# Expert products in four-chunk blocks with column halves, second matrices in 2 KB runs, small steps of selection moved

## The chip, the cores and the metric

The kernel runs on one NeuronCore of one Trainium2 chip. The metric is the device time of one execution in microseconds (us), less is better. The profile is one further execution, recorded instruction by instruction.

## The reference

A gated recurrence runs over 4 sequences of 5056 steps and 256 channels: `f = lb + (1-lb)*sigmoid(f_logit)`, `h = f*h + (1-f)*x`, and every `h` is kept. The 20224 rows of `h` are then tokens of a mixture of 8 experts: `logits = h @ w_gate`, a token goes to the expert with the largest logit, and of each expert's tokens only the 80 with the largest gate probability are kept. A kept token's output row is `gate * (relu(h @ w1[e]) @ w2[e])` (256 to 1024 to 256, float32); every other output row is zero. So 20.7 MB of output are nearly all zeros, 41.4 MB of `x` and `f_logit` are read, and 16.8 MB of expert matrices.

## The kernel before, in words

The order of the instructions on each engine is the order of the program text; nothing is rearranged later. All large transfers are issued from SP's queue, in that order, and with eight completion lanes in turn: a transfer waits until the one eight places ahead has landed.

**The recurrence** (loop at L421) goes through 40 units (10 groups of 512 steps x 4 sequences). A unit loads `f_t` and `x_t` (512 KB each, pool `ld`, four buffers each), takes the sigmoid on ScalarE, multiplies on GpSimd (`enter`, L259), turns both to channels by transposes on TensorE (`to_channels`, L268), makes the decay on ScalarE (L278), scans on VectorE (L286) and makes the logits on TensorE (`logits`, L301), in four column tiles of 32. Zeros of the output are written by copies from an already cleared part of the output to the rest (`clear`, L169), a few among the loads, many after them.

**Selection** (from the end of the loop to L630) makes exponentials (L355), sums on GpSimd (`halved`, L369), masked probabilities (`worth`, L383), transposes of them (`candidates`, L389 and L395), maxima (`peaks`, L400) and then the lists of tokens on VectorE. `busy` (L183) issues matrix products whose result nobody reads. `marks`, `gm` and other tiles lie in the pool `gsm`, which is opened with `ld` and closed with it after the selection's first part. The tile `fresh` in PSUM collects the maxima; two copies by ScalarE (L487, L490) read it before VectorE's search (L560) does.

**Experts** (`experts`, L676). Each expert's two matrices come in halves of 512 KB into a ring of six buffers (`wring`), which takes over the space of `ld` alone: w1 halves at L514 (rows of 2 KB) and w2 halves at L518 (rows of 1 KB). Six are issued before selection's end, with clears among them; each of the other 26 is issued when a half six places ahead has been used up (`more`, L704), 21 of them with a clear of 256 KB behind it. Tokens' columns are gathered out of `h_all` by copies with addresses from registers (L693). Then comes the loop over 64 steps (8 experts x 8 chunks of 128 hidden channels): a step's `hidden` (L725) multiplies a chunk of w1, the stationary operand of 128 columns, with 80 tokens; after four chunks comes a relu (L734); `result` (L740) adds a chunk's product with w2 (256 columns streamed), and in `steps` it runs LAG = 6 steps behind `hidden`, one chunk of each in turn. Each float32 product is two loads and two products on TensorE in the trace. `finish` (L755) scales by the gate, `scatter` (L758) writes 80 rows of the output from GpSimd's queue; scatters wait until all clears are issued and landed. At the very end a register with a flag is loaded on every engine (L804), and a branch (L806) skips a slow exact path.

Of the kernel before, what the change touches and what calls it, by code (L numbers as in the profile page):

```python
# [18 lines left out]
P = 128  # L19
TOP = 8  # L20
# [15 lines left out]
def kernel(  # L36
# [167 lines left out]
    with tc.tile_pool(name="ld", bufs=4) as ld, \  # L204
         tc.tile_pool(name="gsm", bufs=1) as gsm:

        xs, fs, sts, uts, sps, ups, lgs, lss, lts, exs, gms, sms = ({} for _ in range(12))

        zero = gsm.tile([P, ZC], F32, name="zero", tag="ls")

        def setup():
            early = gsm.tile([P, 1], F32, name="early", tag="mx")
            nc.scalar.activation(early, ones, ACT.Sigmoid)
            col_i = gsm.tile([P, P], I32, name="col_i", tag="eq")
            nc.gpsimd.iota(col_i, pattern=[[1, P]], base=0, channel_multiplier=0)
            nc.gpsimd.memset(zero, 0.0)
            col_f = gsm.tile([P, P], F32, name="col_f", tag="gm", bufs=2)
            whole = row_i[:, 0:1]
            for i, (shift, mask) in enumerate(((shift_c, E - 1), (0, C - 1), (2, 1), (0, R - 1),
                                               (0, 2 * R), (0, W - 1))):  # L220
                nc.vector.tensor_scalar(row_i[:, ds(1 + i, 1)], whole, shift, mask,
                                        ALU.arith_shift_right, ALU.bitwise_and)
            nc.vector.tensor_copy(row_f[:, :7], row_i[:, :7])
            res, void = spot_of[:, 0:1], spot_of[:, 1:2]
            nc.vector.scalar_tensor_tensor(out=res, in0=row_f[:, 4:5], scalar=2.0,
                                           in1=row_f[:, 3:4], op0=ALU.mult, op1=ALU.add)
            nc.vector.tensor_tensor(res, res, row_f[:, 5:6], ALU.add)
            nc.vector.tensor_scalar(void, row_f[:, 6:7], float(run(n_grp - 1) // R), GONE,
                                    ALU.is_ge, ALU.mult)
            nc.vector.tensor_copy(col_f, col_i)  # L230
            nc.vector.tensor_scalar(place, col_f[:, :C], row_f[:, 2:3], None, ALU.is_equal)
            nc.vector.tensor_scalar(mine, col_f[:, :E], row_f[:, 1:2], None, ALU.is_equal)
            nc.vector.tensor_scalar(before, col_f, row_f[:, 0:1], None, ALU.is_gt)
            nc.vector.tensor_single_scalar(col_i, col_i, shift_c, op=ALU.arith_shift_right)
            nc.vector.tensor_copy(col_f, col_i)
            nc.vector.tensor_scalar(mates, col_f, row_f[:, 1:2], None, ALU.is_equal)
            nc.vector.tensor_tensor(before, before, mates, ALU.mult)
            busy(psu, 9, "up")
            lb_t = plg.tile([P, DC], F32, name="lb_t", tag="lt")
            nc.tensor.transpose(lb_t, lb, ident[:DC, :DC])  # L240
            nc.vector.tensor_scalar(omlb, lb_t, -1.0, 1.0, ALU.mult, ALU.add)
            nc.vector.tensor_scalar(nomlb, lb_t, 1.0, -1.0, ALU.mult, ALU.add)

        def gates():
            for o in range(DC):
                nc.scalar.activation(wg[:, o], wg[:, o], ACT.Identity, scale=omlb[:, ds(o, 1)])

        def load(n):
            g, b = divmod(n, B)
            fs[n] = ld.tile([P, R, D], F32, name="f_t", tag="f_t")  # L250
            nc.sync.dma_start(out=fs[n], in_=tiles(f_logit, b, g))
            xs[n] = ld.tile([P, R, D], F32, name="x_t", tag="x_t")
            nc.sync.dma_start(out=xs[n], in_=tiles(x, b, g))

        def gate(n):
            s_t = sts[n] = fs.pop(n)
            nc.scalar.activation(s_t, s_t, ACT.Sigmoid, scale=-1.0)  # L257

        def enter(n):  # L259
            u_t = uts[n] = xs.pop(n)  # L260
            (nc.gpsimd if n else nc.vector).tensor_tensor(u_t, sts[n], u_t, ALU.mult)  # L261

        def to_channels(n, src, dst, pool, tag, in_time):
            for o in range(DC):
                ps = dst[n, o] = pool.tile([P, G], F32, name=tag, tag=tag)
                for r in range(R):
                    at = ps[:, r::R] if in_time else ps[:, ds(r * P, P)]
                    nc.tensor.transpose(at, src[n][:, r, ds(o * P, P)], ident)  # L268
            del src[n]

        def columns(n, o):
            g, b = divmod(n, B)
            return h_all[:, b, o, ds(first(g), size(g))]


        def decay(n):
            for o in range(DC):
                nc.scalar.activation(columns(n, o).rearrange("c (p r) -> c p r", r=R),  # L278
                                     sps.pop((n, o)).rearrange("c (r p) -> c p r", r=R)
                                     [:, lead(n // B) // R:],  # L280
                                     ACT.Identity, scale=nomlb[:, ds(o, 1)], bias=1.0)

        def scan(n):
            for o in range(DC):
                h = columns(n, o)
                nc.vector.tensor_tensor_scan(  # L286
                    h, h, ups.pop((n, o))[:, lead(n // B):],
                    columns(n - B, o)[:, size(n // B - 1) - 1:] if n >= B else 0.0,
                    ALU.mult, ALU.add)


        def logits(n):
            g, b = divmod(n, B)
            k = run(g)
            if b == 0:
                lgs[g] = plg.tile([P, B, P], F32, name="lg", tag="lg")
            for o in range(DC):
                h = columns(n, o)
                h = h.rearrange("c (m r two) -> c r m two", r=R, two=2)
                for r in range(R):  # L300
                    nc.tensor.matmul(lgs[g][ds(r * LC, LC), b, :k], wg[:, o], h[:, r],  # L301
                                     start=o == 0, stop=o == DC - 1, skip_group_check=True)

        def aside(g, lo=0, hi=B):
            k = run(g)
            if lo == 0:
                lss[g] = gsm.tile([P, B, P], F32, name="ls", tag="ls")
                if k < P:
                    nc.gpsimd.memset(lss[g][:, :, k:], 0.0)
            nc.scalar.copy(lss[g][:, lo:hi, :k], lgs[g][:, lo:hi, :k])  # L310

        def by_token(g):
            ls = lss.pop(g).rearrange("p b t -> p (b t)")
            lts[g] = plg.tile([P, R, P], F32, name="lt", tag="lt")
            for j in range(R):
                nc.tensor.transpose(lts[g][:, j], ls[:, j::R], ident)

        def shifts(g):
            return cand[:, ds(g * P, P)].rearrange("p (c e) -> p c e", e=E)

        marks = gsm.tile([P, n_grp, C, E], BF16, name="marks")

        full = [P, C, E]

        def maxima(g):
            lg = lts.pop(g).rearrange("p j (r e) -> p (j r) e", e=LC)[:, :, :E]
            mx = gsm.tile([P, C], F32, name="mx", tag="mx")
            nc.vector.tensor_reduce(mx, lg, AX.X, ALU.max)
            nc.vector.tensor_tensor(shifts(g), lg, mx.unsqueeze(2).broadcast_to(full),
                                    ALU.subtract)  # L330

        def shifted(g):
            by_token(g)
            maxima(g)

        def chosen(g):
            eq = gsm.tile([P, C, E], F32, name="eq", tag="eq")
            nc.vector.scalar_tensor_tensor(
                out=eq, in0=shifts(g), scalar=0.0,
                in1=revexp.unsqueeze(1).broadcast_to(full), op0=ALU.is_ge, op1=ALU.mult)  # L340
            pick = gsm.tile([P, C], F32, name="pick", tag="pick")
            nc.vector.tensor_reduce(pick, eq, AX.X, ALU.max)
            return eq, pick

        def mark(g, eq, pick, engine):
            engine.tensor_tensor(marks[:, g], eq, pick.unsqueeze(2).broadcast_to(full),
                                 ALU.subtract)

        def choice(g, engine):
            mark(g, *chosen(g), engine)  # L350

        def exponentials(g0, g1, aside=False):
            sh = cand[:, ds(g0 * P, (g1 - g0) * P)]
            exs[g0] = gsm.tile([P, P], F32, name="ex", tag="ex") if aside else sh
            nc.scalar.activation(exs[g0], sh, ACT.Exp)  # L355
# [531 lines left out]
```

## Time and profile before

| | us |
|---|---|
| median of 3 runs (218.59 to 222.11) | 218.66 |
| the profiled execution, whole | 217.36 |
| its span, first to last instruction | 215.5 |
| TensorE busy / VectorE / GpSimd / ScalarE | 187.8 / 150.7 / 139.1 / 131.4 |
| SP's transfers, packet time as a share of 16 DMA engines | 94.9% |

The span is the stretch that the rows below divide; 1.9 us lie around it. "Busy" is the union of the engine's instructions; a busy TensorE is not TensorE at its peak.

### The profile page before, as it was taken

The numbers are of one execution on the slowest core, as the hardware profiler recorded it, in microseconds if no ns is written. First come the engines' busy times: TensorE is split into PE (matmuls) and PEld (weight loads), VectorE is DVE, ScalarE is ACT, GpSimd is POOL, SyncE is SP. The second block draws the span as 40 slices with busy tenths as digits, with TensorE's granted clock in tenths as the row PEclk, the third lists the DMA queues.
The fourth block names the chain that finished last, engine by engine and source line by source line (L and its number), as shares of the span: only waits on it lengthen the run. The fifth ranks groups of instructions, "written<-read, shape, count | busy, mean of one in ns | idle before, by whom it ended". The sixth has DMA issues, their size and how long they took to land. (4 is left out here: it accounts for less than half of the span.)

```text
span 215.5 us, 5581 instructions
## 1 busy us (share of the span) xinstructions
PE 187.8 (87%) x1878; PEld 158.2 (73%) x1878; DVE 150.7 (70%) x479; ACT 131.4 (61%) x370; POOL 139.1 (65%) x279
## 2 busy tenths in 40 slices
PE   7888689999999999999999767798969899889980
PEld 7677478788878787878788546798857687668850
DVE  5687659999998989898989768945777524510010
ACT  4776588879888888888878623559524443611100
POOL 3484887989898989898888761049966623000741
PEclk9999999999999999999999999999999999999996
DMA  6999999999999999999999899999999999999910
GB/s 218 414 399 416 417 422 415 418 414 426 409 417 414 419 411 417 411 407 424 409 408 395 283 378 363 386 320 400 338 368 410 392 406 405 404 401 397 319 57 24
DMA packets 28825, 80.55 MB, mean 374 GB/s; under 512 B 3058, under 2 KB 11380, under 8 KB 26484
## 3 DMA queue, kind: packets, MB, share of 16 engines
q1 hardware_dynamic: 28400, 79.45, 94.9%
q0 software_dynamic: 384, 0.66, 1.0%
q8 instruction: 17, 0.28, 0.5%
q14 instruction: 20, 0.16, 0.2%
q10 hardware_dynamic: 4, 0.00, 0.0%
HBM read 78.39 MB, written 21.36 MB: 463 GB/s over the span
## 5 line engine op out<-in xcount | busy, mean ns | idle before, releaser
L261 POOL TENSOR_TENSOR x_t<-f_t,x_t 128x1024 f32<-128x1024 f32 x39 | 92.3, 2374 | 16.4 <-DMA x_t<-in_x_dram 11.0
L286 DVE TENSOR_TENSOR_SCAN h_all<-h_all,up 128x512 f32<-128x512 f32 (+1 forms) x80 | 94.7, 1242 | 7.5 <-ACT h_all L278 6.5
L278 ACT ACTIVATE h_all<-sp,nomlb 128x512 f32<-128x512 f32 (+1 forms) x80 | 50.0, 676 | 12.6 <-PE sp L268 12.5
L257 ACT ACTIVATE f_t<-f_t 128x1024 f32<-128x1024 f32 x40 | 42.4, 1061 | 9.3 <-DMA f_t<-in_f_logit_dram 9.2
L268 PE MATMUL up<-ident,x_t 128*128 128x128 f32 x320 | 42.0, 274 | 4.7 <-POOL x_t L261 4.7
L725 PEld LDWEIGHTS h_ps<-xt,w_sb 128*128 128x128 f32 x256 | 36.8, 191 | 12.5 <-DVE xt L701 3.5
L268 PE MATMUL sp<-ident,f_t 128*128 128x128 f32 x320 | 44.6, 283 | 0.1
L268 PEld LDWEIGHTS sp<-ident,f_t 128*128 128x128 f32 x320 | 35.0, 143 | 8.2 <-issue 5.5
L268 PEld LDWEIGHTS up<-ident,x_t 128*128 128x128 f32 x320 | 35.6, 141 | 6.8 <-POOL x_t L261 6.7
L725 PE MATMUL h_ps<-xt,w_sb 128*128 128x80 f32 x256 | 36.8, 269 | 4.0 <-DMA w_sb<-in_moe_w_dram 3.1
L740 PE MATMUL y_ps<-w_sb,hid 128*80 128x256 f32 x128 | 37.3, 381 | 1.3 <-DMA w_sb<-in_moe_w_dram 1.3
L693 POOL COPY xe<-h_all 128x8 uint8 x192 | 26.5, 198 | 16.4 <-issue 6.5
L301 PE MATMUL lg<-h_all,wg 128*32 128x128 f32 (+1 forms) x640 | 26.5, 282 | 5.3 <-ACT ls L310 3.9
L693 DVE COPY xe<-h_all 128x8 uint8 x256 | 20.8, 163 | 11.5 <-issue 11.4
L734 ACT ACTIVATE hid<-h_ps 128x320 f32<-128x320 f32 x16 | 7.0, 436 | 32.3 <-PE h_ps L725 32.3
L301 PEld LDWEIGHTS lg<-h_all,wg 128*32 128x32 f32 x640 | 15.4, 108 | 12.3 <-ACT ls L310 6.8
L693 ACT COPY xe<-h_all 128x8 uint8 x192 | 20.2, 193 | 5.5 <-issue 3.5
L758 POOL DMA_INDIRECT out_dram<-y,goal x8 | 7.5, 938 | 23.8 <-DMA w_sb<-in_moe_w_dram 19.7
L755 DVE TENSOR_SCALAR y<-y_ps,gsl 80x256 f32<-80x256 f32 x8 | 3.8, 477 | 22.6 <-PE y_ps L740 22.6
L183 PE MATMUL warm<-ident 128*128 128x128 f32 x128 | 17.2, 298 | 1.4 <-POOL ident masks.py:199 1.4
L183 PEld LDWEIGHTS warm<-ident 128*128 128x128 f32 x128 | 16.6, 212 | 1.5 <-POOL ident masks.py:199 1.4
L740 PEld LDWEIGHTS y_ps<-w_sb,hid 128*80 128x80 f32 x128 | 14.8, 152 | 2.2 <-issue 1.4
(126 smaller groups left out, 91.9 us busy)
## 6 DMA issues: line engine op xcount, KB each, us to landing
f_t<-in_f_logit_dram SPq DMA_DIRECT2D x40, 512.0 KB, 6.1
x_t<-in_x_dram SPq DMA_DIRECT2D x40, 512.0 KB, 6.5
w_sb<-in_moe_w_dram SPq DMA_DIRECT2D x32, 512.0 KB, 7.7
out_dram<-out_dram SPq DMA_DIRECT2D x34, 256.0 KB, 7.8
out_dram<-out_dram SPq DMA_DIRECT2D x6, 768.0 KB, 11.6
out_dram<-out_dram SPq DMA_DIRECT2D x4, 1024.0 KB, 12.4
out_dram<-zero SPq DMA_DIRECT2D x4, 256.0 KB, 8.4
out_dram<-out_dram SPq DMA_DIRECT2D x2, 512.0 KB, 7.8
```

Source lines behind the costliest of these rows:

```text
L183: nc.tensor.matmul(warm, ident, ident, start=True, stop=True)
L257: nc.scalar.activation(s_t, s_t, ACT.Sigmoid, scale=-1.0)
L261: (nc.gpsimd if n else nc.vector).tensor_tensor(u_t, sts[n], u_t, ALU.mult)
L268: nc.tensor.transpose(at, src[n][:, r, ds(o * P, P)], ident)
L278: nc.scalar.activation(columns(n, o).rearrange("c (p r) -> c p r", r=R), sps.pop((n, o)).rearrange("c (r p) -> c p r", r=R) [:, lead(n // ...
L286: nc.vector.tensor_tensor_scan(h, h, ups.pop((n, o))[:, lead(n // B):], columns(n - B, o)[:, size(n // B - 1) - 1:] if n >= B else 0.0, AL ...
L301: nc.tensor.matmul(lgs[g][ds(r * LC, LC), b, :k], wg[:, o], h[:, r], start=o == 0, stop=o == DC - 1, skip_group_check=True)
L693: copy(xe[:, :, ds(WORD * (k + j), WORD)], pair(v - HOME))
L725: nc.tensor.matmul(HP[e, i][:, c], w[1, e, i][:, o, ds(c * P, P)], XT[e][:, o], start=o == 0, stop=o == DC - 1, skip_group_check=True)
L734: nc.scalar.activation(HID[e][:, ds(i * CH, CH)], HP.pop((e, i)), ACT.Relu)
L740: nc.tensor.matmul(YP[e], HID[e][:, c], w[2, e, c // CH][:, c % CH], start=c == 0, stop=c == FC - 1)
L758: one = nc.gpsimd.indirect_dma_start(out=out, out_offset=bass.IndirectOffsetOnAxis(ap=goal[:, ds(e, 1)], axis=0), in_=Y.pop(e), in_offset= ...
```

## The change

1. `gsm` is allocated at the other end of the memory, so that `ld` can be released right after the loop; `wring` and the first six weight loads stand there in the program text.
2. The exponentials of eight groups are split into two of four groups, the second one unit later; those of group 8 go to a tile of their own and before the loop's end. Their sum comes ahead of `chosen`. Three idle products (`busy(psu, 3)`) go. The two copies out of `fresh` move behind the first search and its replacement.
3. w2 halves: a partition takes two neighbouring rows (`RUN` = 2, 2 KB) where it took one; so chunk `c` of the hidden channels is every second channel of a block of 256, and `hidden` reads every second column of w1.
4. `hidden` makes each product as two of 64 stationary columns, into PSUM partitions 0 to 63 and 64 to 127. `LAG` is 4, and `steps` does a block of four `hidden` and then a block of four `result`. The order of the weight loads stays the same.
5. The flag is loaded during expert 6 and not at the end.

```diff
-    with tc.tile_pool(name="ld", bufs=4) as ld, \
-         tc.tile_pool(name="gsm", bufs=1) as gsm:
+    gsm = tc.alloc_tile_pool(name="gsm", bufs=1, side="right")
+    ld = tc.alloc_tile_pool(name="ld", bufs=4)
...
             elif n == LAST - 2:
-                exponentials(0, OLD)
+            exponentials(0, HALF)
             elif n == LAST - 1:
                 halved(0, HALF)
+            exponentials(HALF, OLD)
+            exponentials(OLD, OLD + 1, aside=True)
...
+    ld.release()
+    wring = ...; the six first weights(*key) with their clears
...
-        best = chosen(OLD)
-        exponentials(OLD, OLD + 1)
         logits(LAST)
         aside(g, B - 1, B)
+    sums(OLD, OLD + 1)
+    best = chosen(OLD)
...
-        sums(OLD, OLD + 1)
         candidates(0)
-        busy(psu, 3, "up")
         candidates(2)
...
         peaks(HALF, fresh)
-        nc.scalar.copy(cand[:, OLD * P:], fresh[:, NP * TOP:])
-        ...
-        nc.scalar.copy(last_of, eighths)
+    gsm.release()
...
-    LAG = FC - 2
+    LAG = CH
+    HC = P // 2
+    RUN = 2
...
-            nc.sync.dma_start(out=t, in_=w2[e][ds(i * FH, FH)].rearrange(
-                "(c p) d -> p c d", p=P))
+            nc.sync.dma_start(out=t.rearrange("p (h j) d -> p h j d", j=RUN),
+                              in_=w2[e][ds(i * FH, FH)].rearrange(
+                                  "(h p j) d -> p h j d", p=P, j=RUN))
...
         nc.vector.match_replace(out=rest, in_to_replace=vals2[:, :TOP], in_values=fresh,
                                 imm_value=GONE)
+        nc.scalar.copy(cand[:, OLD * P:], fresh[:, NP * TOP:])
+        last_of = consts.tile([P, NP], F32, name="last_of")
+        nc.scalar.copy(last_of, fresh[:, TOP - 1:NP * TOP:TOP])
...
+                h, r = divmod(c, RUN)
                 for o in range(DC):
-                    nc.tensor.matmul(HP[e, i][:, c], w[1, e, i][:, o, ds(c * P, P)], XT[e][:, o],
-                                     start=o == 0, stop=o == DC - 1, skip_group_check=True)
+                    for j in range(0, P, HC):
+                        at = (h * P + j) * RUN + r
+                        nc.tensor.matmul(HP[e, i][ds(j, HC), c],
+                                         w[1, e, i][:, o, at:at + (HC - 1) * RUN + 1:RUN],
+                                         XT[e][:, o], start=o == 0, stop=o == DC - 1,
+                                         skip_group_check=True)
...
-                for s in range(lo, hi):
-                    if s < E * FC:
-                        hidden(s)
-                    if 0 <= s - LAG < E * FC:
-                        result(s - LAG)
+                for s in range(lo, min(hi, E * FC)):
+                    hidden(s)
+                for s in range(max(lo - LAG, 0), hi - LAG):
+                    result(s)
...
+                if e == E - 2 and not again:
+                    flag.append(nc.values_load(doubt, ...))
...
-    unsure = nc.values_load(doubt, ...)
+    unsure = flag[0]
```

## Rows read from the trace of the kernel before

**Rows 1.** The page: GB/s moved in 40 equal slices of the span (5.4 us each).
```profile
GB/s 218 414 399 416 417 422 415 418 414 426 409 417 414 419 411 417 411 407 424 409 408 395 283 378 363 386 320 400 338 368 410 392 406 405 404 401 397 319 57 24
```
**Rows 2.** Stretches: length, engines busy (instructions), granted clock, DMA share, GB/s.
```profile
20.00:100.00 80.00, 74.10 (x923) 62.43 (x921) 72.20 (x81) 65.73 (x92) 69.53 (x35) 1.00 1.02 416
142.00:158.00 16.00, 14.82 (x118) 13.71 (x116) 10.80 (x117) 11.04 (x99) 13.29 (x96) 1.00 0.98 344
158.00:192.00 34.00, 30.32 (x202) 24.30 (x202) 17.22 (x174) 14.18 (x105) 13.21 (x96) 1.00 1.05 403
198.00:205.00 7.00, 7.00 (x51) 5.96 (x50) 0.54 (x2) 0.87 (x2) 4.65 (x5) 1.00 0.92 324
```
**Rows 3.** The chain that ended last, in order of time: start us, us, what.
```profile
146.89 2.90 PE h_ps L725 x24
...
151.57 8.91 DMA w_sb<-in_moe_w_dram
...
183.87 8.46 DMA w_sb<-in_moe_w_dram
...
195.21 0.40 PE h_ps L725 x4
...
206.00 3.04 PE y_ps L740 x14
...
209.07 0.49 DVE y L755
```
**Rows 4.** SP's queue in order of time: start us, us, engine, line, operation.
```profile
148.94 0.37 SPq L518 DMA_DIRECT2D w_sb<-in_moe_w_dram  x1
...
161.13 0.52 SPq L169 DMA_DIRECT2D out_dram<-out_dram  x1
162.56 0.37 SPq L518 DMA_DIRECT2D w_sb<-in_moe_w_dram  x1
163.11 0.52 SPq L169 DMA_DIRECT2D out_dram<-out_dram  x1
164.45 0.37 SPq L514 DMA_DIRECT2D w_sb<-in_moe_w_dram  x1
```
**Rows 5.** The last weight load (L518, 199.1 us): its time to landing.
```profile
DMA to landing us min/median/max: 5.8/5.8/5.8
```
**Rows 6.** TensorE's products and weight loads by time; in brackets idle before, and releaser.
```profile
114.86 0.86 PEld L268 LDWEIGHTS sp<-ident,f_t 128*128 128x128 f32 x8 [0.21 <-issue]
115.69 0.56 PEld L316 LDWEIGHTS lt<-ident,ls 128*128 128x128 f32 x4
117.24 0.61 PE L301 MATMUL lg<-h_all,wg 128*32 128x112 f32 x16
120.12 1.02 PE L301 MATMUL lg<-h_all,wg 128*32 128x112 f32 x32
```
**Rows 7.** Selection by time: exponentials, idle products, VectorE's two waits.
```profile
118.96 1.06 ACT L355 ACTIVATE cand<-cand 128x1024 f32<-128x1024 f32 x1
123.32 0.75 PEld L183 LDWEIGHTS warm<-ident 128*128 128x128 f32 x6
124.92 0.91 DVE L400 MAX8 fresh<-cand 128x8 f32<-128x256 f32 x2 [1.12 <-ACT cand L395]
130.45 0.47 DVE L560 MAX8 vals<-fresh 128x8 f32<-128x288 f32 x1 [0.58 <-ACT last_of L490]
```
**Rows 8.** What SP's queue waited for between 115 and 150 us: total, times, longest.
```profile
SPq L514 <- PE up L268: 4.4, 1, 4.4
SPq L518 <- PE h_ps L725: 4.1, 1, 4.1
```
**Rows 9.** The scatters by time, and TensorE's load of the flag (ns).
```profile
206.65 0.91 POOL L758 DMA_INDIRECT out_dram<-y,goal  x1 [0.30 <-issue]
209.82 0.91 POOL L758 DMA_INDIRECT out_dram<-y,goal  x1 [2.27 <-DVE y L755]
L804 PEldq TENSOR_LOAD <-doubt x1: 694/694/694, 206.6 to 206.6; - x1
```

More of the change, by code (lines that the diff above doesn't have):

```diff
@@ new lines, in gates, with load, gate @@
+    def gates():
+        for o in range(DC):
+            nc.scalar.activation(wg[:, o], wg[:, o], ACT.Identity, scale=omlb[:, ds(o, 1)])
+    def load(n):
+        g, b = divmod(n, B)
+        fs[n] = ld.tile([P, R, D], F32, name="f_t", tag="f_t")
+        nc.sync.dma_start(out=fs[n], in_=tiles(f_logit, b, g))
+        xs[n] = ld.tile([P, R, D], F32, name="x_t", tag="x_t")
+        nc.sync.dma_start(out=xs[n], in_=tiles(x, b, g))
+    def gate(n):
+        s_t = sts[n] = fs.pop(n)
+        nc.scalar.activation(s_t, s_t, ACT.Sigmoid, scale=-1.0)
@@ new lines, in enter, with to_channels, columns @@
+    def enter(n):
+        u_t = uts[n] = xs.pop(n)
+        (nc.gpsimd if n else nc.vector).tensor_tensor(u_t, sts[n], u_t, ALU.mult)
+    def to_channels(n, src, dst, pool, tag, in_time):
+        for o in range(DC):
+            ps = dst[n, o] = pool.tile([P, G], F32, name=tag, tag=tag)
+            for r in range(R):
+                at = ps[:, r::R] if in_time else ps[:, ds(r * P, P)]
+                nc.tensor.transpose(at, src[n][:, r, ds(o * P, P)], ident)
+        del src[n]
+    def columns(n, o):
+        g, b = divmod(n, B)
+        return h_all[:, b, o, ds(first(g), size(g))]
@@ new lines, in logits, with aside @@
+    def logits(n):
+        g, b = divmod(n, B)
+        k = run(g)
+        if b == 0:
+            lgs[g] = plg.tile([P, B, P], F32, name="lg", tag="lg")
+        for o in range(DC):
+            h = columns(n, o)
+            h = h.rearrange("c (m r two) -> c r m two", r=R, two=2)
+            for r in range(R):
+                nc.tensor.matmul(lgs[g][ds(r * LC, LC), b, :k], wg[:, o], h[:, r],
+                                 start=o == 0, stop=o == DC - 1, skip_group_check=True)
+    def aside(g, lo=0, hi=B):
+        k = run(g)
+        if lo == 0:
+            lss[g] = gsm.tile([P, B, P], F32, name="ls", tag="ls")
+            if k < P:
+                nc.gpsimd.memset(lss[g][:, :, k:], 0.0)
+        nc.scalar.copy(lss[g][:, lo:hi, :k], lgs[g][:, lo:hi, :k])
@@ new lines @@
+    w_sb = {}
+    for key in order[:RING]:
+        w_sb[key] = weights(*key)
+        clear_some(6 if len(w_sb) > 2 else 5)
+    assert not of_group
+    g = n_grp - 1
+    aside(g, 0, B - 1)
+    logits(LAST)
+    aside(g, B - 1, B)
+    sums(OLD, OLD + 1)
+    best = chosen(OLD)
+    worth(0, 0, 2, nc.gpsimd)
+    worth(2, 0, 2, nc.gpsimd)
+    mark(OLD, *best, nc.gpsimd)
+    candidates(0)
+    candidates(2)
+    by_token(g)
+    halved(HALF, HALF)
+    worth(HALF, HALF, 2, nc.gpsimd)
+    worth(HALF + 2, HALF, 2, nc.gpsimd)
@@ L493, in largest @@
+    worth(OLD, OLD, 1, nc.gpsimd)
+    assert OLD == 8
+    fresh = plg.tile([P, NEW], F32, name="fresh", tag="lg")
+    peaks(0, fresh)
+    maxima(g)
+    exponentials(g, g + 1, aside=True)
+    choice(g, nc.vector)
+    candidates(HALF)
+    sums(g, g + 1)
+    worth(g, g, 1, nc.vector)
+    candidates(HALF + 2)
+    turned(OLD, 1, fresh[:, ds(NP * TOP, P)])
+    turned(g, 1, fresh[:, ds(NP * TOP + P, P)])
+    busy(psu, 10, "up")
+    peaks(HALF, fresh)
+    gsm.release()
     def largest(src, vals, at):
@@ L795, in experts @@
                     nc.vector.tensor_copy(doubt, found)
+                if e == E - 2 and not again:
+                    flag.append(nc.values_load(
+                        doubt, min_val=0, max_val=4 * P,
+                        skip_runtime_bounds_check_because="a sum of 4 * P flags"))
             steps(E * FC, E * FC + LAG)
```

439 lines of the change are left out of this document (180 added, 259 removed).

## The prediction

> **What bounds the kernel now.** I read the slices first. From the second slice to the 37th the transfers run near one level, 405 to 426 GB/s among the loads of `x` and `f_logit`, and below it from slice 23 to 30 [rows 1]. The stretches say that this is a full set of DMA engines and not a lack of requests: share 1.02 at 416 GB/s from 20 to 100 us, 1.05 at 403 from 158 to 192, but 0.98 at only 344 from 142 to 158 and 0.92 at 324 from 198 to 205 [rows 2]. TensorE is busy about nine tenths of the time beside it, at granted clock 1.00 (the 2.4 GHz level) in all of them. Then the chain: TensorE's first expert product is at 146.89, from 151.57 the chain consists of weight loads, each of which waits for the one before; the last of them lands at 183.87 + 8.46 = 192.3. After that it is TensorE without a wait: 0.40 us for the four instructions of a `hidden` step, 3.04 us for the last fourteen of `result`, so 0.43 for the two of a step, 0.84 for both [rows 3]. That is step 48 to the end, 192.3 to 209.04 = 16.7 us. The last load is issued at 199.1 and lands 5.8 us later, at 204.9 [rows 5]. So the transfers pace the steps up to 48, and both engines are close behind one another at the end: a gain needs earlier weights and a shorter tail behind them.
>
> **The change part by part.**
>
> *The pools and the place of the first loads*: nothing. The first load waits for the last `up` transposes (4.4 us of SP's time [rows 8]); the ring lies on `ld`'s space in both kernels, and SP's list has the same order.
>
> *Selection.* Halving the exponentials of 1.06 us lets GpSimd start some 0.5 earlier, but `mark` now waits behind the sum, so GpSimd ends only 0.1 earlier. The idle products (0.75 us) stand ahead of the transposes whose copies VectorE awaits for 1.12 us: about 0.5. The copies out of `fresh`, for which L560 waits 0.58, go behind it: 0.5 [rows 7]. Next late are those copies themselves, covered by the second search. The experts then start 1.0 us earlier, 145.9 (bounds 0 and 1.12 + 0.58 = 1.7). That counts only through SP, which stands 4.1 us before the seventh load for the first ring buffer to be used up [rows 8] and issues at 148.94 [rows 4].
>
> *2 KB runs.* SP issues when the transfer eight places ahead, of the same kind, lands. From clear to w2 half it is 162.56 - 161.13 = 1.43 us, from clear to w1 half 164.45 - 163.11 = 1.34 [rows 4]: 0.09 per half for runs of 1 KB against 2 KB. From the rates: a w1 half, a w2 half and two clears at 403 GB/s on average; were all but the w2 half at 416 [rows 2], that third of the bytes would move at 379 and cost 0.12 more. I take 0.11. Before the 24th load, which lands at 192.3, are eleven w2 halves; eight in the even stretch give 0.9. The first three lie in the poor stretch: at 403 GB/s its 16 us of 344 would take 13.7. These 2.3 us hold their slow runs and a queue that ran short behind SP's wait of 4.1; with the wait some 1.4 shorter (1.0 from selection, 0.4 from faster first blocks) and 2 KB runs I take 0.9 of them. Sum 1.8 us earlier at the 24th load; bounds 0 and 0.9 + 2.3 = 3.2.
>
> The Trainium skill says otherwise ("DMA: Bandwidth & Descriptors", Specifications): transfers of 512 B and more already run at line rate. By it the runs would give nothing and the sum below would be near 1.2, not 3.2; the difference of 0.09 in the issue times speaks against it.
>
> *Column halves.* The trace has no tile of 64 columns, but four of 32: sixteen more `lg` products of 112 columns cost 1.02 - 0.61 = 0.41 us, 0.10 per group of four [rows 6]. The streamed side costs 0.43 / 512 = 0.84 ns a column by `result`, so 94 ns for 112: the four run at once, with 8 ns on top, and their loads are hidden. A `hidden` instruction streams 80 columns, 67 ns, but takes 0.40 / 4 = 100 [rows 3]; loading 128 columns takes 0.86 / 8 = 108 at most, and that binds [rows 6]. A pair of halves loads 64 columns each, 54 ns, hidden behind 67 + 8 = 75. Reading every fourth column takes at most 0.56 / 4 = 140 for 128 [rows 6], so 70 for 64; every second column should lie between, still hidden. Bounds 67 below and 150 above (one half behind the other); I take 75, by the nearest row. Sixteen pairs: 1.20 us where four steps of `hidden` took 1.60.
>
> *Switches.* Between tile forms the load engine idles 0.21 [rows 6]; part of it is hidden. I take 0.15, two per block of four steps (bounds 0 and 0.26). A block: 1.20 + 4 x 0.43 + 0.30 = 3.22, now 3.36. The loads' pace is two halves and two clears, 3.9 us, so TensorE still waits for them in the middle.
>
> *The tail.* From the 24th load's landing TensorE now needs 16.7. After: four blocks, 12.9, and the last four results, 1.72 + 0.15: 14.8 without waits. Loads 25 to 27 still come every 1.9 us behind clears, and the result of block 48 and of block 52 wait for theirs, 0.5 us in all: 15.3. Gain 1.4 (at a pair of 100 and switches of 0.26, none). The later loads are no longer held by ring buffers, which blocks free sooner, and LAG 4 leaves four results after the last landing, 1.72 us.
>
> *The flag.* The load on TensorE takes 0.69 us, now between expert 6's results and expert 7's first products; results of 1.72 us are in the queue, so nothing shows unless they wait, at most 0.7. On GpSimd scatter 6 stands behind it; the scatters follow one another every 0.30 + 0.91 = 1.21 us and have 209.82 - 206.65 - 1.21 = 1.96 of slack before the last [rows 9]. Nothing is gained at the end: that load was off the chain.
>
> Sum: 1.8 + 1.4 = 3.2. The profiled execution took 217.36, 1.3 less than the median; against itself 214.2, against the median 218.66 - 3.2 = **215.4**.
>
> **Rivals.**
>
> *Halves one behind the other.* If the second half's load or product waits for the first, a pair takes 2 x 75 = 150 ns, sixteen 2.4 us, a block 4.42, more than the loads' pace of 3.9. TensorE becomes the bound from the first block: 145.9 + 2.4 + 15 x 4.42 + 1.87 = 216.5 in place of 209.04, so 226.1. It decides from 121 ns a pair (no gain in all); 2% is reached at 138. Against it: the four tiles of `lg` at once. The Trainium skill has a rule that leads here ("TensorE: Matmul & The Clock Gate", Part 3, the mechanism): a weight load overlaps a running product only when the row group differs, and the halves share theirs. The 0.10 us per group in `lg`, which also shares its rows, contradicts it. 9%.
>
> *The runs give nothing and the poor stretch stays.* Only the tail's gain, less some 0.2 for its slower w2 halves: 1.2, 217.5. For it: the bytes are the same, and a share over 1 bounds by the slowest engine. 20%.
>
> *The poor stretch fills altogether.* 3.2 + 1.6: 4.8, 213.9. For it: the wait of 4.1 and the runs explain the stretch together. 26%.
>
> My forecast has 45%.
>
> **Numbers.** Forecast 215.4. The range 213.4 to 217.9 leaves out the serial halves and the ends. What this kernel can tell from no change is about 2%, 4.4 us: faster is below 214.3. Of the filled stretch some two thirds fall there, of the forecast a fifth: 0.27. Slower is the serial case with little else: 0.10. Within: 0.63.
>
> **What would show it.** `h_ps` pairs at 75 ns and blocks of sixteen in 1.2 us; clear to w2 at 1.34; the stretch from 142 at 380 GB/s or more; first expert product near 145.9; last landing to end of results 1.7 to 2.5 us. It is wrong if pairs exceed 120 ns, if switches take over 0.3, if TensorE's granted clock falls in the longer pauses of selection, or if w2 halves land no faster.

## The result, and the profile after

The changed kernel takes 220.35 us (median of 13 runs) against 218.89 for the kernel before beside it: ratio 1.0083, 95% interval 1.0057 to 1.0109. The ratio leaves out slow executions, over 1.5% above the fastest of the same kernel, so it is not quite the quotient of the medians. The forecast was 215.4. The profiled execution took 221.51 us with a span of 219.7; the one of before took 217.36 with 215.5. So the two profiles lie 4.2 us apart and the medians 1.5: the profile of before lies 1.5 below its kernel's median, the other 1.2 above.

Read the chip's side first. Stretches of the changed kernel, columns as in [rows 2]:

```profile
20.00:100.00 80.00, 74.25 (x922) 62.37 (x921) 71.96 (x81) 66.91 (x93) 69.32 (x35) 1.00 1.03 416
124.00:130.00 6.00, 3.41 (x15) 2.31 (x14) 4.07 (x12) 1.19 (x4) 3.22 (x8) 0.82 1.02 414
130.00:136.00 6.00, 6.00 (x48) 6.00 (x48) 5.79 (x16) 3.57 (x15) 1.22 (x4) 0.89 1.02 370
142.00:158.00 16.00, 13.13 (x181) 10.93 (x180) 11.11 (x118) 11.43 (x102) 13.42 (x97) 1.00 1.01 344
158.00:192.00 34.00, 29.15 (x330) 20.49 (x330) 16.77 (x172) 13.59 (x104) 13.10 (x96) 0.95 1.04 410
206.00:210.00 4.00, 3.17 (x10) 1.84 (x11) 0.48 (x1) 0.44 (x1) 0.95 (x2) 0.55 0.14 41
```

The even stretch of loads runs at 410 GB/s in place of 403, the poor one still at 344 [rows 2]. TensorE's granted clock is 0.82 and 0.89 in selection, and 0.55 at the end, between its two levels of 1.2 and 2.4 GHz (0.5 and 1.00).

SP's queue in the even stretch (start us, us, engine, line, operation; L472 loads a `w1` half, L476 a `w2` half), to be read beside [rows 4]:

```profile
175.90 0.37 SPq L472 DMA_DIRECT2D w_sb<-in_moe_w_dram  x1
176.50 0.52 SPq L169 DMA_DIRECT2D out_dram<-out_dram  x1
177.79 0.37 SPq L476 DMA_DIRECT2D w_sb<-in_moe_w_dram  x1
178.40 0.52 SPq L169 DMA_DIRECT2D out_dram<-out_dram  x1
179.71 0.37 SPq L472 DMA_DIRECT2D w_sb<-in_moe_w_dram  x1
...
183.51 0.37 SPq L472 DMA_DIRECT2D w_sb<-in_moe_w_dram  x1
```

Clear to `w2` half is 177.79 - 176.50 = 1.29, down from 1.43. But the step behind it, `w2` to clear, is 0.61 and was 163.11 - 162.56 = 0.55 [rows 4]: part of what the half saves comes back at once. The 24th load is the one of 183.51; it lands at 191.96, 0.4 earlier than before.

Now the chain's last stretch, TensorE by time (start us, us, line, tiles, count, idle before and releaser), which answers [rows 3]:

```profile
146.36 1.33 PE L734 MATMUL h_ps<-xt,w_sb 128*64 128x80 f32 x32 [0.56 <-DVE xt L707]
...
158.07 3.18 PE L751 MATMUL y_ps<-w_sb,hid 128*80 128x256 f32 x8 [2.38 <-DMA w_sb<-in_moe_w_dram]
...
197.31 1.93 PE L751 MATMUL y_ps<-w_sb,hid 128*80 128x256 f32 x8 [0.31 <-DMA w_sb<-in_moe_w_dram]
199.17 1.33 PE L734 MATMUL h_ps<-xt,w_sb 128*64 128x80 f32 x32
200.43 1.95 PE L751 MATMUL y_ps<-w_sb,hid 128*80 128x256 f32 x8
202.31 1.22 PE L734 MATMUL h_ps<-xt,w_sb 128*64 128x80 f32 x24
204.61 0.31 PE L734 MATMUL h_ps<-xt,w_sb 128*64 128x80 f32 x3 [1.08 <-issue]
205.32 0.23 PE L734 MATMUL h_ps<-xt,w_sb 128*64 128x80 f32 x1 [0.40 <-issue]
206.03 0.35 PE L734 MATMUL h_ps<-xt,w_sb 128*64 128x80 f32 x3 [0.48 <-issue]
206.75 0.29 PE L734 MATMUL h_ps<-xt,w_sb 128*64 128x80 f32 x1 [0.37 <-issue]
207.47 6.49 PE L751 MATMUL y_ps<-w_sb,hid 128*80 128x256 f32 x16 [0.43 <-issue]
```

The block that starts at 199.17 is what was forecast: sixteen pairs in 1.26 us (to 200.43), results in 1.9. The next breaks off after 24 of 32 products. The rest comes in small groups about 0.71 us apart, and what ended each pause is "issue": TensorE waited for nothing that the profile shows, no semaphore and no load. That it had no instruction to run is the reading I take from this; no row shows the supply itself. The clock falls, and the last sixteen results take 6.49 us. And on GpSimd, the scatters, which answer [rows 9]:

```profile
198.80 1.13 POOL L768 DMA_INDIRECT out_dram<-y,goal  x1 [21.33 <-DMA w_sb<-in_moe_w_dram]
200.24 0.92 POOL L768 DMA_INDIRECT out_dram<-y,goal  x1 [0.30 <-issue]
...
206.84 0.92 POOL L768 DMA_INDIRECT out_dram<-y,goal  x1 [0.80 <-issue]
214.75 0.92 POOL L768 DMA_INDIRECT out_dram<-y,goal  x1 [7.00 <-DVE y L765]
```

All seven held-back scatters are issued one behind the other from 198.8, when the last clear has landed. The eighth waits for the results and comes at 214.75, 4.9 us later than before.

TensorE is not the only engine that is late there. ScalarE's `relu` (L745) and VectorE's `finish` (L765) in the same stretch:

```profile
203.26 0.44 ACT L745 ACTIVATE hid<-h_ps 128x320 f32<-128x320 f32 x1 [5.77 <-PE y_ps L751]
206.08 0.48 DVE L765 TENSOR_SCALAR y<-y_ps,gsl 80x256 f32<-80x256 f32 x1 [9.82 <-remote]
209.12 0.44 ACT L745 ACTIVATE hid<-h_ps 128x320 f32<-128x320 f32 x1 [5.43 <-remote]
```

"Remote" stands where the profile finds no instruction of this core as the releaser. The first `relu` reads products that were through at 199.17 + 1.33 = 200.5, so it is 2.8 us late; `finish` reads results that were through at 200.43 + 1.95 = 202.4, so it is 3.7 late.

### The profile page after: what moved, and what is told of

Read it like the earlier page. It is cut to its first block, busy times and chain, and to the rows that moved or that the text cites. A ratio compares the mean times of both kernels' runs of the same rounds, so it can differ in the third digit from the quotient of the medians.

```text
span 219.7 us, 6080 instructions
## 1 busy us (share of the span) xinstructions
PE 187.3 (85%) x2128; PEld 150.4 (68%) x2128; DVE 150.3 (68%) x479; ACT 131.2 (60%) x371; POOL 139.3 (63%) x279
## 4 chain that ended last, share of the span: by engine, by line
DMA 35%; PE 32%; POOL 11%; issue 8%; ACT 5%; DVE 5%; POOLq 1%; SPq 1%; DVEq 0%; ACTq 0%
DMA w_sb<-in_moe_w_dram 21%; DMA x_t<-in_x_dram 11%; PE sp L268 10%; PE up L268 9%; PE lg L301 7%; POOL x_t L261 5%; DMA f_t<-in_f_logit_dram 3%; ACT h_all L278 3%; POOL out_dram L768 2%; ACT ls L310 2%; POOL xe L699 1%; DVE at L601 1%; PE lt L316 1%; PE h_ps L734 1%; ACT f_t L257 1%
## 5 line engine op out<-in xcount | busy, mean ns | idle before, releaser
L268 PE MATMUL sp<-ident,f_t 128*128 128x128 f32 x320 | 44.0, 280 | 1.5 <-ACT h_all L278 1.4
L751 PE MATMUL y_ps<-w_sb,hid 128*80 128x256 f32 x128 | 34.8, 422 | 8.3 <-DMA w_sb<-in_moe_w_dram 5.5
L268 PEld LDWEIGHTS sp<-ident,f_t 128*128 128x128 f32 x320 | 34.3, 140 | 10.0 <-issue 5.5
L751 PEld LDWEIGHTS y_ps<-w_sb,hid 128*80 128x80 f32 x128 | 19.9, 165 | 19.0 <-issue 7.9
L745 ACT ACTIVATE hid<-h_ps 128x320 f32<-128x320 f32 x16 | 7.0, 436 | 35.1 <-PE h_ps L734 23.9
L734 PEld LDWEIGHTS h_ps<-xt,w_sb 128*64 128x64 f32 x512 | 19.6, 140 | 8.5 <-issue 7.2
L734 PE MATMUL h_ps<-xt,w_sb 128*64 128x80 f32 x512 | 22.7, 239 | 2.9 <-issue 2.3
L765 DVE TENSOR_SCALAR y<-y_ps,gsl 80x256 f32<-80x256 f32 x8 | 3.8, 478 | 28.8 <-PE y_ps L751 19.0
L183 PEld LDWEIGHTS warm<-ident 128*128 128x128 f32 x122 | 17.1, 227 | 1.5 <-POOL ident masks.py:199 1.4
```

What stands on the lines that cost most here:

```text
L183: nc.tensor.matmul(warm, ident, ident, start=True, stop=True)
L734: nc.tensor.matmul(HP[e, i][ds(j, HC), c], w[1, e, i][:, o, at:at + (HC - 1) * RUN + 1:RUN], XT[e][:, o], start=o == 0, stop=o == DC - 1, ...
L745: nc.scalar.activation(HID[e][:, ds(i * CH, CH)], HP.pop((e, i)), ACT.Relu)
L751: nc.tensor.matmul(YP[e], HID[e][:, c], w[2, e, c // CH][:, c % CH], start=c == 0, stop=c == FC - 1)
```

## The experiments

The question: what stalls TensorE from 203.5 on? Ratios are to the kernel before, run beside it on the same chip, with 95% intervals.

**e1: the flag's load back at the end.**

```
-                if e == E - 2 and not again:
-                    flag.append(nc.values_load(doubt, ...
...
-    unsure = flag[0]
+    unsure = nc.values_load(doubt, min_val=0, max_val=4 * P, ...
```

> The flag is read into the engines' registers after the last scatter again, as before; all else as in the changed kernel, in which TensorE's last block of sixteen pairs starts at 202.31, gets its instructions from 203.30 in groups 0.71 us apart and ends at 206.9, and the last sixteen results then take 6.49 us. Theory F (the register load in the middle of TensorE's list makes the list run dry): the last block takes 1.3 us, the results end near 207.2 in place of 213.96, time 213 to 215. Theory S (the last stretch of TensorE's list ahead of the branch is supplied slowly, whatever stands in it): the groups 0.7 us apart are still there, time 219.5 to 221.

221.20 us, 1.0086 (1.0049 to 1.0124). The last block breaks off after 22 products. Theory F falls.

**e2 and e3: TensorE's list 12 and 64 instructions longer.**

```
-        busy(psu, 20, "up")
+        busy(psu, 17, "up")          # e3: 4
+        busy_halves(psu, 6, "up")    # e3: 32; 64 columns each
```

> Three of the idle products of 128 columns in selection become six of 64 columns: as much streaming, but TensorE's list is 12 instructions longer ahead of the experts, so that the branch stands 12 instructions behind a multiple of 256 and not just ahead of one. Theory S1 (the slow stretch belongs to the piece of 256 instructions in which the branch stands): only the last dozen instructions are slow, as in the kernel before, the last block takes about 1.3 us, time 213 to 216. Theory S2 (the slow stretch is a fixed number of instructions ahead of the branch) and theory F: as the changed kernel, 219.5 to 221.

> The same with sixteen products made thirty-two: 64 instructions more, as much streaming. Theory S1: the last 64 instructions, from inside the last block on, are slow, so the groups 0.7 us apart are there, with the same or a few more instructions: 219.5 to 222. Theory S2 and theory F: the same stretch as in the changed kernel, 219.5 to 221. If it is the place of the multiple of 256 within the last block that stalls, it moves 64 instructions earlier and the last block is whole: 213 to 216.

220.30 us, 1.0087 (1.0053 to 1.0121), and 219.90, 0.9994 (0.9957 to 1.0031). The block breaks off after 21 and 23 products: where the list stands against the multiples of 256 of the expectations does not matter. S1 falls. Both stall alike, yet their ratios are 0.9% apart, so a single ratio is not to be trusted much below that.

**e4: whole chunks of 128 columns in the first product.**

```
-                    for j in range(0, P, HC):
-                        at = (h * P + j) * RUN + r
-                        nc.tensor.matmul(HP[e, i][ds(j, HC), c],
-                                         w[1, e, i][:, o, at:at + (HC - 1) * RUN + 1:RUN], ...
+                    at = h * P * RUN + r
+                    nc.tensor.matmul(HP[e, i][:, c],
+                                     w[1, e, i][:, o, at:at + (P - 1) * RUN + 1:RUN], ...
```

> The first product takes whole chunks of 128 columns again (strided by two), one instruction where two halves stood; 1024 instructions fewer on TensorE's list, so the branch keeps its place against the multiples of 256. Theory of the prediction for the halves: a block takes 1.60 in place of 1.20 us, 0.4 more; TensorE waits for weights in the middle, so only the tail is later, by some 1.2 us without the stall. Theory S: the slow stretch now covers eight steps of the first product or less, each instruction of which brings twice the work, so the stall shrinks by half or more: 216 to 219. Theory that only halves stall: no groups 0.7 us apart at all, about 215.5.

218.76 us, 0.998 (0.9937 to 1.0023). TensorE's list is 512 instructions shorter by the traces (6080 and 5568 in all), not 1024. No groups in the block, but the last eight results stand idle for 2.56 us:

```profile
208.97 0.44 ACT L744 ACTIVATE hid<-h_ps 128x320 f32<-128x320 f32 x1 [6.72 <-remote]
```

```profile
209.46 1.95 PE L750 MATMUL y_ps<-w_sb,hid 128*80 128x256 f32 x8 [2.56 <-ACT hid L744]
```

The `relu` ahead of them runs 3.8 us late, for the products it reads were through near 205.2. So without the halves the groups are gone, the loss is smaller, and what is left of it sits on ScalarE, whose list this edit did not touch.

**e5, e6, e7: is it the branch?** e5 and e7 leave out the branch and the fallback behind it (changed kernel, kernel before); e6 puts idle products ahead of it.

```
-    with tc.If(unsure > 0):          # e5, e7: and all in it
...
     unsure = flag[0]
+    busy(psl, 16, "rivals")          # e6
```

> The changed kernel without the branch and all that stands behind it (the fallback for doubtful selections, which these inputs don't enter, and the loads of the flag into the engines' registers); nothing that runs before it is altered. Theory S2 (TensorE's last fifty or so instructions ahead of the branch are supplied slowly because of the branch): no groups 0.7 us apart, the last block takes 1.3 us, the last sixteen results 3.5, they end near 207.0 in place of 213.96, time 213 to 215. Theory E (what is slow is the end of TensorE's list, or the time at which the transfers run out, branch or no branch): the groups are still there, 219 to 221.

> The changed kernel with sixteen idle products (64 instructions) on TensorE between the last result and the branch. Theory S2: the slow stretch moves onto the idle products, the last block takes 1.3 us and the results end near 207.5, but the branch stands behind 64 slow instructions of some 0.1 to 0.18 us, so the end comes at 217 to 224, as TensorE's list decides it. Theory E of a fixed time: the last block is as slow as in the changed kernel, the results end at 212 to 214, time 221 to 228.

> The kernel before without the branch, the fallback behind it and the loads of the flag. Its results end at 209.04 without a gap, the branch on TensorE ends at 210.97 and the last scatter's transfer later, so both theories expect 217 to 219, at most 1 us below the kernel before. Against the changed kernel without the branch it prices the rest of the change: by S2 some 3 us (1.4 to 1.6%), by E nothing or a loss.

218.90 us, 1.0006 (0.9972 to 1.004); 221.01, 1.0103 (1.0061 to 1.0145); 218.20, 0.9965 (0.9924 to 1.0006). e7's profiled execution (220.81 us) shows that the order of the kernel before is not proof against the row either. Its `relu` ran 3.0 us behind the end of its products, and the last eight results waited for it:

```profile
210.88 0.44 ACT L734 ACTIVATE hid<-h_ps 128x320 f32<-128x320 f32 x1 [5.84 <-remote]
```

```profile
211.37 3.07 PE L740 MATMUL y_ps<-w_sb,hid 128*80 128x256 f32 x8 [2.21 <-ACT hid L734]
```

e6, TensorE's end by time:

```profile
201.52 1.05 PE L734 MATMUL h_ps<-xt,w_sb 128*64 128x80 f32 x23
203.56 0.39 PE L734 MATMUL h_ps<-xt,w_sb 128*64 128x80 f32 x4 [1.00 <-issue]
204.99 0.36 PE L734 MATMUL h_ps<-xt,w_sb 128*64 128x80 f32 x4 [1.04 <-issue]
...
206.44 5.41 PE L751 MATMUL y_ps<-w_sb,hid 128*80 128x256 f32 x16 [0.49 <-issue]
211.68 2.51 PE L183 MATMUL warm<-ident 128*128 128x128 f32 x21
```

With 64 instructions more behind it the block breaks off after 23 products, where the changed kernel has 24, and the idle products themselves run freely. Without a branch (e5) it breaks off after 24. The Trainium skill ("Runtime: NRT & Kernel Launch", Instruction fetch mechanics) says that instructions are fetched ahead in sequence, and that a taken branch breaks this where its target has not been fetched. The stall stands ahead of the branch and stays without it (e5), so that rule does not explain it. S2 falls.

**What all these have in common is a time.** In e1 to e3, e5 and e6 the pause begins 4.6 to 4.7 us behind the first scatter of the row (in the changed kernel, 198.80 to 203.5). In the changed kernel TensorE runs without a pause again from 207.47 on, 1.4 us behind the end of the sixth scatter (205.12 + 0.92).

**e9 and e10: the changed kernel and the kernel before without the scatters of experts 0 to 6.**

```
             def scatters(e):
+                if e < E - 1 and not again:
+                    return
```

> The changed kernel without the scatters of experts 0 to 6 (their rows are not written; all products are made, and the last scatter is as it was). So far the slow stretch of TensorE's list has stayed at the same place in time whatever stood ahead of it or behind it, and it ended 1.2 to 1.5 us after the last of seven scatters that GpSimd issues one behind the other from 198.8 on. Theory G (that row of scatters starves TensorE's instruction supply): no groups 0.7 us apart, last block 1.3 us, results 3.5 to 4 us, ending near 207.2; time 213 to 215. Theory E (the end of TensorE's list): as the changed kernel, 219 to 221.

> The kernel before without the scatters of experts 0 to 6. Its results end at 209.04 without a gap, so theory G expects no more than 0.5 us from it: 217.5 to 219, and against the changed kernel with the same left out some 1.4 to 2.5% (the gain of 3.2 us that was forecast, or the 1.8 that the trace leaves). Theory E: the same here, no difference between the two.

215.49 us, 0.9807 (0.976 to 0.9854), and 218.77, 0.9959 (0.9925 to 0.9992). e9 by time:

```profile
199.75 1.33 PE L736 MATMUL h_ps<-xt,w_sb 128*64 128x80 f32 x32
201.02 1.95 PE L753 MATMUL y_ps<-w_sb,hid 128*80 128x256 f32 x8
202.90 1.33 PE L736 MATMUL h_ps<-xt,w_sb 128*64 128x80 f32 x32
204.16 3.68 PE L753 MATMUL y_ps<-w_sb,hid 128*80 128x256 f32 x16
```

No pause, granted clock 1.00, results in 3.68 us in place of 6.49; `relu` and `finish` come at 201.19 and 203.01, within 0.1 us of the end of what they read. The row of scatters is needed for the stall. With the same scatters left out of both, the change gains 218.77 - 215.49 = 3.3 us; the kernel before loses at most 0.75% to its row.

**e11: the row held until the last results.**

```
-                if not zeros:
+                if not zeros and e == E - 1:
```

> The changed kernel with the scatters of experts 0 to 6 held until the last expert's results are done, so that the row of scatters comes behind TensorE's work. Theory G: the last block takes 1.3 us and the results end near 207.2, then eight scatters of 1.22 us follow, the last at 216.5, time 221 to 223. Theory E: the last block as slow as in the changed kernel, results at 212 to 214, the last scatter near 222, time 226 to 229.

221.41 us, 1.0079 (1.0036 to 1.0121). The edit did not hold the row: a scatter waits for its own `y` and the clears alone, so GpSimd issued the first at 199.35, and the stall is there, from 204.0. It does not test what it was made for.

**e12: four clears more before the seventh load.**

```
-    clear_some(6 if len(w_sb) > 2 else 5)
+    clear_some(10 if len(w_sb) == RING else 6 if len(w_sb) > 2 else 5)
```

> The changed kernel with four more clears behind the sixth weight load, where SP stands 4 us for the first ring buffer; the last four loads that had a clear behind them have none. The last clear then lands some 7 us earlier, and the row of scatters with it, ahead of the last block. Theory G: no slow stretch in the last two blocks, results end at 206 to 208; time 213 to 216. Theory E: the slow stretch stays, 218 to 221.

220.19 us, 1.002 (0.999 to 1.0051). TensorE waited 8.4 us for weights after the first blocks, so the time says nothing for G. But the stall has moved to the block before the last two:

```profile
199.88 1.06 PE L734 MATMUL h_ps<-xt,w_sb 128*64 128x80 f32 x24
201.89 0.54 PE L734 MATMUL h_ps<-xt,w_sb 128*64 128x80 f32 x8 [0.96 <-issue]
...
204.47 1.33 PE L734 MATMUL h_ps<-xt,w_sb 128*64 128x80 f32 x32 [0.16 <-issue]
...
207.62 1.33 PE L734 MATMUL h_ps<-xt,w_sb 128*64 128x80 f32 x32
```

GpSimd issued four scatters in a row from 196.26 to 201.04; the pause lies at 200.9 to 201.9, and the blocks behind it, beside a pair and single scatters, are whole. From the first scatter to the pause it is 4.7 us again, as in e11 and e16: the row came 2.5 us earlier and took the pause with it. Three weight loads were still issued from 200.49 on, and the transfers moved 281 to 307 GB/s from 202 to 208, so the end of the other transfers is not what it takes.

**e16 and e17: what of the row, and anywhere?** e16 sends the rows of the seven scatters past the output's end, so that none is written. e17 leaves those scatters out and puts a row of seven such dropped ones in the middle.

```
+                rows = goal if again or e == E - 1 else nowhere      # e16
...
+                    if e == 4 and not again:                         # e17
+                        row_of_scatters(e - 1)
```

> The changed kernel with the row numbers of the scatters of experts 0 to 6 set past the end of the output: GpSimd issues the same seven scatters at the same times, and their rows are dropped (not written). Theory G1 (the data of the scatters starves TensorE's instruction supply): no stretch with groups 0.7 us apart, 215 to 216, as without the scatters. Theory G2 (GpSimd's own part of a scatter, 0.92 us each, does it): the slow stretch stays, 219 to 221.

> The changed kernel without the scatters of experts 0 to 6, and with a row of seven dropped scatters (row numbers past the end, into a spare buffer) on GpSimd in the middle of the experts, behind the result of expert 3, near 181 us. TensorE's list is in mid-stream there, the transfers are at full rate, and nothing ends. Theory G2 (a row of scatters, wherever it stands, starves TensorE's instruction supply, from some 4 us behind its first to some 1.3 us behind its last): between 184 and 192 us a block of sixteen pairs shows groups 0.7 us apart, and the last block at 203 none. Theory E2 (the row only hurts together with the end of the transfers or of the list): no such groups anywhere, all blocks 1.3 us.

222.43 us, 1.0173 (1.0118 to 1.0229): the block breaks off after 22 products with 0.08 MB on the scatters' queue in place of 0.66. Their data is not needed. e17: 217.04 us, 0.999 (0.9964 to 1.0016), its row and TensorE beside it:

```profile
182.25 1.13 POOL L784 DMA_INDIRECT spare<-y,nowhere  x1 [9.60 <-DVE y L770]
...
189.76 0.91 POOL L784 DMA_INDIRECT spare<-y,nowhere  x1 [0.31 <-issue]
```

```profile
185.48 1.33 PE L739 MATMUL h_ps<-xt,w_sb 128*64 128x80 f32 x32
187.51 1.93 PE L756 MATMUL y_ps<-w_sb,hid 128*80 128x256 f32 x8 [0.70 <-DMA w_sb<-in_moe_w_dram]
189.50 1.33 PE L739 MATMUL h_ps<-xt,w_sb 128*64 128x80 f32 x32
```

All blocks are whole. So a row of scatters alone does not stall TensorE: G2, as I put it, falls, and what else is needed stays open. The profile lists transfers of instructions, 16 KB each, on a queue of their own. In the changed kernel one lies among the row's packets (202.8), in e17 they lie on either side (185.0 and 196.6, packets from 186 to 195). That explains nothing yet: in e12, which stalls, it lies just ahead of them (198.9), and in the kernel before and in e18, which do not, one lies among them (204.6, 203.5). Another difference was not tested: in e17 TensorE waits some 0.7 us, mostly for weights, ahead of each eight results beside the row, while in the changed kernel and in e12 it has run 6 us without a wait when it stalls (from 197.31 and 194.88 on).

The times of e16 and e17 are not to be set against the others. Their experts start near 148.5, 2.1 us later than in the changed kernel; no run says which part of the edit did that.

**e8, e13, e14, e15, e18: the parts, and a better version.** e13 is the kernel before with 2 KB runs alone; e8 the changed kernel with the products of before; e14 is e4 without the scatters of experts 0 to 6; e15 is e8 with idle products in selection, e18 is e15 with two clears behind later loads.

```
     by_token(g)
+    busy(psu, 7, "up")                                               # e15, e18
...
-                    clear_some(1)
+                    clear_some(0 if len(late) in (16, 12) else 1)    # e18
```

> The kernel before with second matrices in 2 KB runs alone (the first product reads every second column to match). By the prediction's term (0.11 us per second half, eleven halves, and part of the poor stretch) the 24th load lands 0.9 to 1.4 us earlier than 192.3, time 217.3 to 218, ratio 0.993 to 0.996. By the changed kernel's trace (a clear behind each half takes back what the half saves, 3.81 in place of 3.84 us per two halves and two clears) it lands 0.2 to 0.4 earlier, ratio 0.998 to 1.000.

> The changed kernel with the products of the kernel before: whole chunks of 128 columns, a step of the second product behind each step of the first, ten of the first ahead, the weights loaded in that order; second matrices in 2 KB runs, load buffers, selection and flag as changed. By the prediction's terms the 24th load lands 1.8 us earlier than before and the tail is as before: 216.9. By what the changed kernel's trace showed (24th landing 0.4 earlier, experts 0.5): 218.2 to 218.6, ratio 0.997 to 1.000. S2: the slow stretch is covered by the products queued on TensorE as in the kernel before, so no gap at the end.

> The changed kernel with whole chunks of 128 columns in the first product and without the scatters of experts 0 to 6. Against the same omission with column halves (215.5) it prices the halves where nothing starves TensorE: 16 products take some 1.9 us in place of 1.26, four blocks behind the 24th load, so 2.0 to 2.6 us later: 217.3 to 218. By theory G no gap at the end.

> The kernel with the products of before in the changed frame (217.7) and seven idle products on TensorE behind the last transposes of the logits, where it stands 1.7 us with nothing to do before its clock falls. Theory C (the gap in selection is what lets the clock fall, 0.62 to 0.88 of 2.4 GHz between 124 and 136 us in every changed version): the clock stays near 1.00 there, the experts start 0.3 to 0.6 earlier, time 217.1 to 217.6. Otherwise, if the products only push the transposes behind them: experts at the same time or later, 217.6 to 218.3.

> The best version so far (products of before, 2 KB runs, idle products in selection: 216.68) with two of the clears behind weight loads moved behind later loads. The last clear and with it the row of scatters come some 1 to 2.5 us later, the weights before them up to 1.2 us earlier. If the 0.87 us that TensorE's last eight products still wait is the row's doing, they wait 0.3 or less: 215.8 to 216.4; if the row now holds the last scatter instead, 216.5 to 217.5.

e13: 217.31 us, 0.9938 (0.9909 to 0.9967); experts at 146.85 as before, 24th load at 191.20, 1.1 earlier. e8: 217.74 us, 0.9915 (0.9873 to 0.9957); last eight results wait 0.80 us. e14: 215.43 us, 0.9856 (0.9792 to 0.992); from the 24th landing to the end of the results 208.13 - 191.76 = 16.4 us, against 207.84 - 192.61 = 15.2 in e9, so the halves save 1.1 us of it in these two executions. The two times don't tell the kernels apart, where the expectation had 2 us or more. e15: 216.68 us, 0.9907 (0.9868 to 0.9947); clock 1.00 from 124 to 136, experts at 146.12 in place of 146.71. e18: 216.68 us, 0.9969 (0.994 to 0.9998), on a chip where the kernel before took 217.21: the wait of 0.87 is gone, results end at 207.57, but the row now ends at 209.85 with the last scatter in it. e15 beats both kernels; that the clears' move adds to it is not shown, nor that the idle products add to e8 (0.9907 beside 0.9915).

## Why the prediction was wrong

*The step that failed is the tail*, which I counted from TensorE's products, loads and weights alone. "Four blocks, 12.9, and the last four results" did hold: where no row runs beside it, 15.2 us were measured against 15.3. With the row it is 213.96 - 191.96 = 22.0. I had the row in front of me and charged its 1.21 us per scatter to GpSimd's queue only [rows 9]; it holds up TensorE, ScalarE and VectorE as well. How it does that stays open.

The other half of the step is that I charged the halves nothing for doubling the first product's instructions: 64 in a block's 1.26 us, loads included, where the kernel before needs 32 in 1.60. With whole chunks TensorE showed no groups beside the same row (e4, e8, e13, e15, e18, kernel before), so the groups go with the halves. That the number of instructions is the reason is argued and not shown, and whole chunks were not free of loss: their last results waited for a late `relu`, 2.56 us in e4, 0.80 in e8, none in the profile of before [rows 3] and in e18.

The ledger between the two profiled executions (not between the medians): without the stall the results would end 4.94 us (e9) behind the last block's start, 202.31 + 4.94 = 207.25, 1.8 earlier than before; the stall and the lower clock add 213.96 - 207.25 = 6.7; the end behind them is 0.7 shorter (219.7 - 213.96 against 215.5 - 209.03). Sum 4.2, as 221.51 - 217.36. Of the 6.7, the slower last results, at the lower clock, have 6.49 - 3.68 = 2.8.

*Column halves*: right in size, 1.26 us for sixteen pairs, 79 ns a pair against 75. Whole blocks follow one another in 3.15 (199.75 to 202.90 in e9) against 3.22. The rival "one behind the other" is out.

*2 KB runs*: the 1.8 us for selection and runs at the 24th load was mis-sized; the changed kernel's profile gives 0.4. By themselves (e13) the runs came out 1.1 earlier, nearly all of it in the poor stretch, from the seventh load's issue to that of the fourteenth: 14.43 us (148.99 to 163.42), before 15.51 (148.94 to 164.45). But single executions of that stretch differ by more: 14.90 in e8 and 16.10 in e15, both with 2 KB runs, 18.64 in e10 with 1 KB. The even stretch gives 0.2 in e13, where I had 0.9. There I read one interval of SP's queue, and over whole periods of two halves and two clears the gain is 3.84 - 3.78 = 0.06 per `w2` half (172.35 to 183.87 before and 172.17 to 183.51 after, three periods each), not 0.11. The Trainium skill ("DMA: Bandwidth & Descriptors", Specifications) has 512 B as enough for line rate. Only e13's time speaks against it, with an interval below 1 as a whole; the traces do not settle it, and the rival "runs give nothing" is not out.

*Selection*: 0.5 earlier in this pair of profiles, not 1.0. Single executions spread: 146.09 to 147.09 with the changed selection (e1 to e6, e8, e9, e11, e12, e14), 146.85 in e13 and 147.75 in e10 with the one of before. The clock fell to 0.82 and 0.89, which I had named among what would make it wrong, but it fell with the selection of before too (0.94 and 0.78 in e13, 0.82 and 0.61 in e10); idle products in that gap keep it at 1.00 (e15). The earlier start bought little in any case: SP's wait went from 4.1 us to 2.8, the poor stretch stayed at 344 GB/s with a full share, and TensorE waited 2.38 us for weights at 155.7. So the rival "poor stretch fills" is out (its 1.6 us more should have been 1.4 by my own bound of 3.2).

*The flag*: as forecast, nothing (e1). One reading was off with nothing resting on it: among the loads of `x` and `f_logit` two slices lie below 405 GB/s, at 399 and 395 [rows 1].

The sum of 3.2 us is what the change earns without the row (3.3), and that is in part luck. In e9 the 24th load lands at 192.61, no earlier than before (192.3), so the 1.8 us of that term came from elsewhere: the end behind the results is 0.6 shorter there (213.7 - 207.84 against 215.5 - 209.03), and the experts of e10, with which the 3.3 is formed, start late, at 147.75 in its profile. Only the tail's 1.4 was earned as forecast, 16.7 - 15.2 = 1.5.

## What to carry to other kernels

Before recasting the work near a kernel's end, look at what else runs in that stretch, above all scatters issued in a row, and charge them to every engine and not only to the queue that issues them. A change that halves each product's work doubles the number of instructions; here only the version with the halves broke into groups, so price it in a run that has the row beside it. A gain read from one interval of a queue, or from one pair of executions, is checked on whole periods and on other runs.

## What the runs showed of the hardware

In every version with column halves and the row of indirect transfers at the end, TensorE's products broke off 4.6 to 4.7 us behind the row's first scatter, with and without data, branch or flag, and went on in small groups about 0.7 us or twice that apart (in e12, with four scatters in the row, after one pause). Without the row all blocks ran at 1.33 us (e9), and beside a row in the middle too (e17). With whole chunks there were no groups, but in e4, e7, e8, e13 and e15 ScalarE's `relu` came late beside the row, by 1.6 us in e8 and 3.8 in e4. In the changed kernel the granted clock was 0.55 from 206 to 210 us, the lower of its levels for most of it, where e9 had 1.00; the single pause of 0.96 us in e12 left it at 1.00.
